# Moving output transfers, weight conversion and broadcasts between queues in an LSH-attention + MoE kernel

## The chip, the cores and the metric

The kernel runs on one core of one Trainium2 chip. The metric is device time in microseconds (us), lower is better. Before the change three timed runs gave 1048.49, 1049.14 and 1049.36 us, so a median of 1049.14 us. The five engines each execute their own instructions in order: PE (TensorE, matmuls), DVE (VectorE), ACT (ScalarE), POOL (GpSimd) and SP (SyncE, which here only issues DMA transfers).

## The reference, cut to what matters

```python
q_bits = (np.einsum('bhsd,dk->bhsk', q, proj) > 0)       # 6 hash bits per row, k likewise
mask   = q_bucket[:, :, :, None] == k_bucket[:, :, None, :]
scores = np.where(mask, scale * q @ k.T, -1e9)           # B=4, H=8, S=768, D=64
attn   = softmax(scores)
x      = (attn @ v)  -> (B*S, H*D) = (3072, 512)
h      = x @ w_in                                        # 512 -> 2048
g      = h * np.clip(h + 3.0, 0.0, 6.0) / 6.0
out    = g @ w_out                                       # 2048 -> 512
```

All inputs are 8-byte floats on the host for the two weights and float32 for q, k and v. Products are formed from a high and a low part, so most matmuls occur in twos or threes.

## The kernel before, in words

**Attention.** There are 4 x 8 = 32 heads, and 6 steps (blocks of 128 rows) to a head, so 192 steps `k`. In step `k` PE transposes the probabilities of block `k` (L347, six transposes into `pt`), multiplies an older block by the values (L384, L385), and computes the scores of block `k + 3` (`lead`, L315, L318). DVE takes the minimum of the scores (`lowest`, L325) and makes the low parts of the transposed probabilities (L371); ACT does the exponential (L337) and the high parts (L370). Where `k` is a multiple of 6, `lead` also hashes the next head: six matmuls `z` (L275 to L277) and the bits on DVE (L286).

**Preparing the next head.** Where `k % 6 == 3`, `split_qk` (L244) rounds the raw q and k on POOL (L263) into `q1`. Three DMA transfers on SP then copy halves of `q1` to `k2`, `q2` and `k1` (`kk<-qq`, `qq<-qq`, `kk<-qq`, L264 to L266), and POOL makes the two low parts (L267, L268). The hash three steps later reads all of these. `split_v` (L301, L302) comes at `k % 6 == 5`, and `scale_q` (L242), which multiplies the freshly loaded raw q for the head after, at `k % 6 == 1`. The two accumulating output transfers of each head are issued by POOL itself (`add`, L391) at `k % 6 == 4` and `1`.

**Outputs.** `output` (L394) copies an accumulated `acc` to `y` on ACT (L412), and SP writes it to the DRAM scratch `xs` (L416): 64x512 for the first four blocks of a head, 64x256 for the last two. A transfer on SP waits, in SP's order, for the copy that fills its source. The order of PE, DVE, ACT and POOL is the order of the code; the order on SP is chosen by the scheduler by its own estimate of when each source is ready, unless `tc.issue_after` names a transfer that must stand ahead.

**Weights.** The 32 pieces of the weights (`wr`, 128x512 values of 8 bytes each, handled as pairs of 32-bit words) are turned into a high and a low float part by `convert` (L159), a generator whose every `yield` ends one step: a shift on DVE (L179), a merge of two words on DVE (L181), an absolute value with scale on ACT (L186) followed by a clamp, a second merge on DVE (L194), then the high part on ACT (L199) and four low parts of 128 columns on POOL (L203). The clamp is on POOL (L189) during attention and on DVE (L192) once the feed-forward part runs. `early` (L603) has a table that says at which step `k` each of the first four pieces takes its next conversion step; the other 28 are converted in `first_ffn` (L640).

**Batch 0 is alone.** Steps 0 to 51 (48 steps of batch 0 and the first of batch 1) run without feed-forward work beside them. From step 34 on `early` also loads and normalises the finished heads for the feed-forward part: `invert`, `widen` (L572: a broadcast of 128x768 on POOL, three times), `divide` (two PE transposes `rt` and a DVE multiply, L446, L449), and transfers `load0` (`xr<-xs`, L564). `first_ffn` then runs the feed-forward part of batch 0 (48 units of 12 matmuls `h` and 6 matmuls `po`, L488 to L512). After it the remaining heads run with the feed-forward work of the batches before woven in.

## Time and profile before

| what | value |
|---|---|
| median of three timed runs | 1049.14 us |
| the profiled execution's own time | 1045.8 us |
| its span | 1043.9 us |
| mean granted PE clock | 0.996 |
| PE busy | 1009.8 us |
| DVE, ACT, POOL busy | 687.0, 584.5, 477.3 us |
| steps 12 to 47 of batch 0 | 42.73 to 144.74 us of the span |
| feed-forward of batch 0, about | 160 to 299 us |

A row of the timeline reads: start in us from the span's start, duration, engine and line, operation, output<-inputs, shape, count, and in brackets the idle time of the engine just before and what ended it. A row on windows gives for a stretch its length and then the busy time and instruction count of each engine, the granted PE clock (1.00 is full), and the share of the DMA engines. The waits view sums idle time by who waited and for whom.

### The profile page before, as it was taken

What the parts mean: (1) busy time and instruction counts of PE and PEld (TensorE: products, weight loads), DVE (VectorE), ACT (ScalarE), POOL (GpSimd) and SP (SyncE); (2) the same over time, 40 slices, a digit from 0 to 9 for tenths busy, and PEclk for the clock granted to TensorE, in tenths of its full rate; (3) what the DMA queues carried; (4) which work ended last, traced back from release to release, by engine and by line L of the source; (5) the groups of instructions that cost most, each with busy time, mean ns of one, the idle gap of its engine ahead of it and who ended that gap; (6) DMA issues with size and microseconds to landing.
All of it is one profiled execution on the core that took longest, in us unless ns stands there. A gap on an engine that the chain in (4) does not pass through costs nothing.

```text
span 1043.9 us, 18989 instructions
## 1 busy us (share of the span) xinstructions
PE 1009.8 (97%) x6846; PEld 926.0 (89%) x6846; DVE 687.0 (66%) x1441; ACT 584.5 (56%) x1308; POOL 477.3 (46%) x529
## 2 busy tenths in 40 slices
PE   8988889999999999999999999999999999999998
PEld 7977878888889998899999999999999999899996
DVE  6997888898769998766566665656665663333332
ACT  6876775556578887654554555454455462333332
POOL 5786742666537776544445444544454232200100
PEclk9999999999999999999999999999999999999999
DMA  3645559300035554322222232232232011101000
GB/s 97 150 112 130 147 150 360 142 1 1 6 110 125 115 121 134 89 62 59 60 63 63 52 95 55 43 79 64 60 93 46 15 37 28 41 1 41 1 22 20
DMA packets 47412, 80.68 MB, mean 77 GB/s; under 512 B 5924, under 2 KB 27812, under 8 KB 47320
## 3 DMA queue, kind: packets, MB, share of 16 engines
q1 hardware_dynamic: 42840, 73.98, 24.1%
q0 software_dynamic: 4480, 5.51, 4.6%
q8 instruction: 54, 0.88, 0.4%
q14 instruction: 38, 0.31, 0.1%
HBM read 41.95 MB, written 18.09 MB: 58 GB/s over the span
## 4 chain that ended last, share of the span: by engine, by line
PE 86%; DVE 6%; issue 2%; ACT 2%; DMA 2%; POOL 2%; SPq 0%; DVEq 0%; POOLq 0%; ACTq 0%
PE pt L347 11%; PE h L489 8%; PE h L488 8%; PE h L490 8%; PE po L512 7%; PE po L510 7%; PE po L511 7%; PE acc L384 6%; PE acc L385 6%; PE s L315 6%; PE s L318 6%; DVE pl L371 2%; PE z L277 1%; DVE p L325 1%; DMA qq<-qq 1%
## 5 line engine op out<-in xcount | busy, mean ns | idle before, releaser
L325 DVE TENSOR_SCALAR_CACHE_REDUCE p<-s 128x768 f32<-128x768 f32 x192 | 183.6, 956 | 102.2 <-PE pt L347 96.3
L371 DVE TENSOR_TENSOR pl<-pt,ph 128x384 fp32r<-128x384 f32 x376 | 191.9, 551 | 51.0 <-ACT ph L370 49.0
L370 ACT CAST ph<-pt 128x384 fp32r<-128x384 f32 x376 | 165.8, 481 | 64.7 <-PE pt L347 52.8
L337 ACT ACTIVATE p<-p,m 128x768 f32<-128x768 f32 x192 | 179.8, 936 | 11.1 <-DVE p L325 10.7
L497 ACT ACTIVATE g<-h,three 128x256 f32<-128x256 f32 x192 | 91.6, 477 | 153.6 <-PE h L490 131.2
L347 PE MATMUL pt<-ident,p 128*128 128x128 f32 x1152 | 162.9, 275 | 11.9 <-DVE pl L371 10.3
L503 POOL TENSOR_TENSOR gl<-g,gh 128x256 fp32r<-128x256 f32 x96 | 74.6, 777 | 203.0 <-DVE gh L502 159.4
L347 PEld LDWEIGHTS pt<-ident,p 128*128 128x128 f32 x1152 | 136.9, 141 | 31.3 <-issue 7.4
L498 DVE SCALAR_TENSOR_TENSOR g<-g,h 128x256 f32<-128x256 f32 x192 | 80.7, 420 | 114.7 <-ACT g L497 112.1
L384 PE MATMUL acc<-ph,vv 128*128 128x256 f32 x564 | 152.1, 302 | 1.0 <-DVE pl L371 1.0
L488 PE MATMUL h<-xh,w 128*128 128x256 f32 x512 | 147.7, 289 | 1.2 <-ACT y L412 1.2
L489 PE MATMUL h<-xl,w 128*128 128x256 f32 x512 | 143.3, 280 | 0.3 <-DVE xl L480 0.3
L490 PE MATMUL h<-xh,w 128*128 128x256 f32 x512 | 143.2, 280 | 0.0
L385 PE MATMUL acc<-pl,vv 128*128 128x256 f32 x564 | 140.5, 282 | 0.0
L510 PE MATMUL po<-w,gh 128*128 128x512 f32 x320 | 126.7, 396 | 0.1
L512 PE MATMUL po<-w,gl 128*128 128x512 f32 x320 | 126.5, 395 | 0.0
L511 PE MATMUL po<-w,gh 128*128 128x512 f32 x320 | 126.1, 394 | 0.0
L384 PEld LDWEIGHTS acc<-ph,vv 128*128 128x128 f32 x564 | 107.0, 190 | 2.2 <-DVE pl L371 1.9
L385 PEld LDWEIGHTS acc<-pl,vv 128*128 128x128 f32 x564 | 107.4, 190 | 0.0
L315 PE MATMUL s<-kk,qq 76*128 76x384 f32 x384 | 101.7, 346 | 2.3 <-ACT kk L291 1.5
L318 PE MATMUL s<-kk,qq 128*128 128x384 f32 x384 | 100.7, 343 | 0.0
L488 PEld LDWEIGHTS h<-xh,w 128*128 128x128 f32 x512 | 96.4, 188 | 3.8 <-ACT y L412 2.4
(137 smaller groups left out, 2025.2 us busy)
## 6 DMA issues: line engine op xcount, KB each, us to landing
raw<-in_qkT SPq DMA_DIRECT2D x32, 384.0 KB, 3.4
kk<-qq SPq DMA_DIRECT2D x62, 192.0 KB, 3.2
wr<-in_w_in SPq DMA_DIRECT2D x16, 512.0 KB, 9.6
wr<-in_w_out SPq DMA_DIRECT2D x16, 512.0 KB
vr<-in_v SPq DMA_DIRECT2D x32, 192.0 KB, 3.0
qq<-qq SPq DMA_DIRECT2D x31, 192.0 KB, 3.1
out<-ob SPq DMA_DIRECT2D x11, 512.0 KB, 3.0
xr<-xs SPq DMA_DIRECT2D x9, 512.0 KB
```

Source lines behind the costliest of these rows:

```text
L325: nc.vector.tensor_scalar(out=pr_[:], in0=s[:, :, :HW], scalar1=CAP, scalar2=None, op0=ALU.min, op1=ALU.min, accum_out=m[:],)
L337: nc.scalar.activation(pr_[:], pr_[:], AF.Exp, bias=m[:], scale=-1.0, accum_out=sms[b][:, t, h : h + 1])
L347: nc.tensor.transpose(pt[:, x], probs[g][0][:, c, x * P : (x + 1) * P], ident[:])
L371: nc.vector.tensor_sub(lo[:, :, w], pt[:], hi[:, :, w].bitcast(F32))
L384: nc.tensor.matmul(acc[:], lhsT=vv[:, kt], rhs=hi[:, x], start=(kt == 0), stop=False)
L385: nc.tensor.matmul(acc[:], lhsT=vv[:, kt], rhs=lo[:, x], start=False, stop=(kt == KT - 1))
L488: nc.tensor.matmul(hp[:], lhsT=wi[:, 0, wc], rhs=xh, start=(cc == 0), stop=False)
L489: nc.tensor.matmul(hp[:], lhsT=wi[:, 0, wc], rhs=xl, start=False, stop=False)
L490: nc.tensor.matmul(hp[:], lhsT=wi[:, 1, wc], rhs=xh, start=False, stop=(cc == NCC - 1))
L510: nc.tensor.matmul(po[u], lhsT=gh[:, us], rhs=wo[:, 0], start=(fc == 0), stop=False)
L511: nc.tensor.matmul(po[u], lhsT=gh[:, us], rhs=wo[:, 1], start=False, stop=False)
L512: nc.tensor.matmul(po[u], lhsT=gl[:, us], rhs=wo[:, 0], start=False, stop=(fc == NFC - 1))
```

## The change

Four edits go together; the numbers of matmuls and of DMA transfers stay the same.

1. Every output transfer on SP (L416) is placed behind the last of the three `q1` copies of the head split most recently (`tc.issue_after(copied.ins)`).
2. The conversion table of batch 0 has steps only at `k % 6` equal to 0, 2 and 3, two of them (0 and 2) with DVE or POOL work. Three pieces are converted whole, with seven steps, and the fourth only up to its second step; `first_ffn` starts it at its third (`stage = {WA - 1: 2}`). The high part on ACT and the four low parts on POOL become two separate steps during attention.
3. The clamp is always on DVE.
4. `widen` runs on ACT instead of POOL, at steps 36, 37 and 38 instead of 36, 38 and 42.

```diff
@@ convert
-            nc.scalar.activation(hf, hf, AF.Abs, scale=2.0 ** -112)
-        early = not ffn_on
-        if early:
-            nc.gpsimd.tensor_single_scalar(hf, hf, E_HI, op=ALU.min)
         yield
-        if not early:
-            nc.vector.tensor_single_scalar(hf, hf, E_HI, op=ALU.min)
-            yield
+        nc.vector.tensor_single_scalar(hf, hf, E_HI, op=ALU.min)
+        yield
...
         nc.scalar.copy(w[:, 0], hf)
+        if not ffn_on:
+            yield
@@ split_qk
         dma(out=k1[:D].bitcast(F32), in_=q1[D:].bitcast(F32))
+        copied = last
@@ output
-            dma(out=to, in_=outs[i][r])
+            with tc.issue_after(copied.ins):
+                dma(out=to, in_=outs[i][r])
@@ widen
-        nc.gpsimd.tensor_copy(
+        nc.scalar.copy(
             over[cc].rearrange("p (k h d) -> p k h d", k=KT, h=P // D),
@@ early
-        for n, ks in enumerate(((9, 10, 12, 13, 14), (15, 16, 18, 19, 20), (21, 22, 24, 25, 26), (27, 28, 30, 31, 32))):
+        for n, ks in enumerate(((12, 14, 15, 18, 20, 21, 24), (24, 26, 27, 30, 32, 33, 36), (36, 38, 39, 42, 44, 45, 50), (48, 50))):
...
-        put(37, div(0, 0))
-        put(38, lambda: widen(1), div(1, 0))
+        put(37, lambda: widen(1), div(0, 0))
+        put(38, lambda: widen(2), div(1, 0))
@@ first_ffn
-        stage = {}
+        stage = {WA - 1: 2}
```

**On SP, around the split at step 21.** Before, in SP's own order (`y_0` is a head's first four blocks, `y_2` its last two; `kk_975` and `qq_976` belong to the head being split):

```order
L76 DMA vr_863<-in_v 128x384
L76 DMA wr_914<-in_w_in 128x4x256
L76 DMA xs_125<-y_0_988 64x512
L76 DMA kk_975<-qq_976 64x768
L76 DMA qq_976<-qq_976 64x768
L76 DMA kk_975<-qq_976 64x768
L76 DMA raw_1051<-in_qkT 128x768
```

With the change, at the same place (the same head is `kk_959`, `qq_960`):

```order
L76 DMA xs_125<-y_2_899 64x256
L76 DMA wr_902<-in_w_in 128x4x256
L76 DMA kk_959<-qq_960 64x768
L76 DMA qq_960<-qq_960 64x768
L76 DMA kk_959<-qq_960 64x768
L76 DMA xs_125<-y_0_972 64x512
L76 DMA raw_1033<-in_qkT 128x768
```

The 64x512 output moved from ahead of the three copies to behind them; the load of the next raw head stays behind it. The same holds at the splits of steps 27 and 33. At the split of step 45 the transfer that moved behind the copies is `xr<-xs`.

**On POOL, from the split at step 21 to that at step 27.** Before:

```order
L268 TENSOR_TENSOR qq_976<-raw_827,qq_976 64x768
L391 DMA xs_125<-y_2_910 64x256
L301 CAST vv_1048<-vr_863 128x6x64
L302 TENSOR_TENSOR vv_1048<-vr_863,vv_1048 128x6x64
L189 TENSOR_SCALAR wr_914<-wr_914 128x512
L391 DMA xs_125<-y_0_988 64x512
L242 TENSOR_SCALAR raw_1051<-raw_1051 64x768
L203 TENSOR_TENSOR w_990<-wr_914,w_990 128x128 x4
L263 CAST qq_1200<-raw_1051 128x768
```

With the change (line numbers are shifted by up to 6: L272 is L268 of before, L395 is L391, L305 and L306 are L301 and L302, L266 is L263):

```order
L272 TENSOR_TENSOR qq_960<-raw_817,qq_960 64x768
L395 DMA xs_125<-y_2_899 64x256
L305 CAST vv_1030<-vr_853 128x6x64
L306 TENSOR_TENSOR vv_1030<-vr_853,vv_1030 128x6x64
L203 TENSOR_TENSOR w_652<-wr_471,w_652 128x128 x4
L395 DMA xs_125<-y_0_972 64x512
L242 TENSOR_SCALAR raw_1033<-raw_1033 64x768
L266 CAST qq_1181<-raw_1033 128x768
```

The clamp is gone, and the four low parts of a piece no longer stand right ahead of the split; they stand behind `split_v`, and in every second head only.

**On DVE, from the bits at step 12 on.** Before (L194 is the second merge of the first piece, L179 the shift of the second):

```order
L286 TENSOR_SCALAR qq_528<-z_641,thr,val 44x768
L325 TENSOR_SCALAR p_667,m_666<-s_648 128x768
L371 TENSOR_TENSOR pl_0_632<-pt_0_657,ph_0_631 128x3x128
L371 TENSOR_TENSOR pl_1_636<-pt_1_661,ph_1_635 128x3x128
L194 SCALAR_TENSOR_TENSOR wr_471<-wr_471 128x512
L325 TENSOR_SCALAR p_702,m_701<-s_680 128x768
L371 TENSOR_TENSOR pl_0_712<-pt_0_692,ph_0_711 128x3x128
L371 TENSOR_TENSOR pl_1_716<-pt_1_696,ph_1_715 128x3x128
L325 TENSOR_SCALAR p_739,m_738<-s_719 128x768
L371 TENSOR_TENSOR pl_0_712<-pt_0_729,ph_0_711 128x3x128
L371 TENSOR_TENSOR pl_1_716<-pt_1_733,ph_1_715 128x3x128
L179 TENSOR_SCALAR wr_690<-wr_690 128x512
```

With the change (L290 is the bits, L329 is L325, L375 is L371, L181 is the shift and L183 the first merge of the first piece):

```order
L290 TENSOR_SCALAR qq_528<-z_638,thr,val 44x768
L181 TENSOR_SCALAR wr_471<-wr_471 128x512
L329 TENSOR_SCALAR p_664,m_663<-s_645 128x768
L375 TENSOR_TENSOR pl_0_629<-pt_0_654,ph_0_628 128x3x128
L375 TENSOR_TENSOR pl_1_633<-pt_1_658,ph_1_632 128x3x128
L329 TENSOR_SCALAR p_698,m_697<-s_677 128x768
L375 TENSOR_TENSOR pl_0_708<-pt_0_688,ph_0_707 128x3x128
L375 TENSOR_TENSOR pl_1_712<-pt_1_692,ph_1_711 128x3x128
L183 SCALAR_TENSOR_TENSOR wr_471<-wr_471 128x512
```

The shift moved from the step in which POOL splits (step 15) to behind the bits (step 12), and merges stand at step `k % 6 == 2` alone.

## The prediction

> **What bounds the kernel now.** I read the page first (PE busy 97% of the span), so only PE's idle time and time at a lower clock can be won. Then the windows, one per head of batch 0, cut at the first transposes of a head. The columns are the stretch, its length, busy time of PE, weight loads, DVE, ACT, POOL, the PE clock, DMA share.

> ```profile
> core 0 of [0], span 1043.9 us
> core 0: us, PE busy (x) PEld busy (x) DVE busy (x) ACT busy (x) POOL busy (x), PEclk, DMA share, GB/s
> 28.84:42.73 13.89, 13.79 (x104) 13.28 (x102) 13.22 (x28) 11.81 (x27) 9.49 (x9) 1.00 0.62 152
> 42.73:58.57 15.84, 13.97 (x104) 13.29 (x102) 15.38 (x31) 13.04 (x29) 13.20 (x14) 1.00 0.55 135
> 58.57:74.41 15.84, 13.96 (x104) 13.30 (x102) 15.28 (x30) 13.17 (x29) 13.16 (x14) 1.00 0.43 99
> 74.41:92.79 18.38, 14.44 (x104) 13.28 (x102) 15.37 (x31) 13.02 (x29) 13.14 (x14) 1.00 0.57 146
> 92.79:111.50 18.71, 15.83 (x103) 14.74 (x102) 13.26 (x29) 13.16 (x30) 11.59 (x12) 0.91 0.45 115
> 111.50:129.42 17.92, 15.40 (x111) 14.03 (x110) 14.05 (x32) 12.46 (x28) 13.55 (x14) 1.00 0.67 171
> 129.42:144.74 15.32, 14.44 (x109) 13.63 (x107) 14.57 (x31) 13.17 (x31) 12.10 (x12) 1.00 0.54 138
> 318.69:332.35 13.66, 13.66 (x104) 13.29 (x102) 12.58 (x26) 11.88 (x28) 9.84 (x9) 1.00 0.51 120
> ```

> The same work takes 13.66 us in an undisturbed head of batch 1 (last row) and 13.89 in the second head of batch 0, but 15.3 to 18.7 in the six heads in which weights are converted and batch 0 is normalised. These six heads last 102.01 us together; six of 13.66 would be 81.96. What PE waited for from 42.73 to 160 us, by the waits view:

> ```profile
> PE pt L347 <- DVE pl L371: 8.2, 10, 1.6
> PE z L276 <- DMA kk<-qq: 6.1, 4, 2.0
> PE z L277 <- DMA qq<-qq: 1.8, 3, 0.7
> ```

> So there are two causes of like size: DVE is late with the low parts, and the hash waits for the copies of `q1`. The second has its explanation on POOL and SP (step 27; POOL, then SP, then PE):

> ```profile
> 84.79 1.75 POOL L203 TENSOR_TENSOR w<-wr,w 128x128 fp32r<-128x128 f32 x4 [1.97 <-PE pt L347]
> 86.50 0.82 POOL L263 CAST qq<-raw 128x768 fp32r<-128x768 f32 x1
> 92.67 0.47 SPq L76 DMA_DIRECT2D xs<-y  x1
> 93.24 0.54 SPq L76 DMA_DIRECT2D kk<-qq  x1
> 96.56 0.39 PE L276 MATMUL z<-kk,pjh 128*108 128x384 f32 x1 [2.02 <-DMA kk<-qq]
> ```

> The copy's source was ready at 87.32, yet SP issued it at 93.24, right behind an output that had to wait for its `y`. On top of that L263 started 1.75 us late, behind the low parts of a weight piece. DVE's own lateness shows here:

> ```profile
> 47.90 2.14 POOL L242 TENSOR_SCALAR raw<-raw 64x768 f32<-64x768 f32 x1
> 48.70 0.68 DVE L194 SCALAR_TENSOR_TENSOR wr<-wr 128x512 uint32<-128x512 uint32 x1
> 50.87 0.41 PE L347 MATMUL pt<-ident,p 128*128 128x128 f32 x2 [0.32 <-DVE pl L371]
> 53.17 1.84 POOL L267 TENSOR_TENSOR kk<-raw,qq 64x768 fp32r<-64x768 f32 x1
> 53.25 2.04 DVE L179 TENSOR_SCALAR wr<-wr 128x512 uint32<-128x512 uint32 x1
> 165.35 0.42 DVE L179 TENSOR_SCALAR wr<-wr 128x512 uint32<-128x512 uint32 x1
> 169.97 0.42 DVE L192 TENSOR_SCALAR wr<-wr 128x512 f32<-128x512 f32 x1
> ```

> The shift L179 takes 2.04 us when it starts beside POOL's L267, and 0.42 us at 165.35, where POOL has nothing. The clamp on DVE (L192) also takes 0.42 us alone. A single merge of 0.68 us costs PE 0.32 us two steps on.

> **Heads of steps 12 to 35.** They took 15.84 + 15.84 + 18.38 + 18.71 = 68.77 us. Of that go:
> - the waits for copies at steps 24 and 30 (parts of the 6.1 and 1.8 above): the copies are issued when L263 ends, some 6 us before the hash, and L263 no longer stands behind L203. At steps 12 and 18, where the copies were ahead already, no wait for them is in the view, so nothing is next there at once;
> - the long shifts: they move to where POOL has no split, so 0.42 instead of 2.04 us;
> - a third of the DVE steps: two a head (0.42 and 0.68, together 1.10 us) instead of three (2.04, 0.68 and 0.68, together 3.40).

> The nearest head is that of 28.84 (13.89 us), which holds one shift and one merge and no late copy. If every merge costs PE its 0.32 us and the short step is hidden, a head takes 13.98; if the short step costs as much again, 14.3; if both lie in DVE's slack, 13.66. I take 14.0, near the measured head: 56.0 us, so **-12.8** (bounds -11.6 and -14.1).

> In this sum the clock counts too:

> ```profile
> 97.10:100.50 3.40, 3.00 (x11) 2.88 (x12) 1.09 (x1) 0.00 (x0) 2.10 (x2) 0.57 0.63 144
> ```

> Granted clock 0.57 for 3.40 us, right after the 2.02 us wait of 96.56, costs some 1.5 us. I let it go with the wait. [...] The row has the drop right behind the longest gaps and nowhere else in these heads, so I follow the row.

> Merges at `k % 6 == 2` may meet POOL's L242. The row of 48.70 lies wholly inside L242's (47.90 to 50.04) and took 0.68 us, as does a merge alone; I count nothing. [...]

> **Head of steps 36 to 41** (17.92 us). The copies' wait goes here as well. Added: three `widen` on ACT at the ends of steps 36 to 38, and the first merge and an absolute value. The nearest rows for their cost:

> ```profile
> L189 POOL TENSOR_SCALAR wr<-wr 128x512 f32<-128x512 f32 x4 | 6.3, 1566 | 7.0 <-ACT wr L186 7.0
> L575 POOL COPY lent<-rc 128x768 f32<-128x768 f32 x3 | 2.5, 818 | 0.0
> L337 ACT ACTIVATE p<-p,m 128x768 f32<-128x768 f32 x38 | 35.7, 938 | 6.1 <-DVE p L325 5.9
> L186 ACT ACTIVATE wr<-wr 128x512 f32<-128x512 f32 x4 | 2.7, 674 | 0.0
> L446 PE MATMUL rt<-ident,lent 128*128 128x128 f32 x12 | 2.3, 271 | 0.0
> ```

> An ACT pass over 768 columns is 0.94 us, so 2.8 us go to ACT within three steps; POOL had 0.82 each in its idle time, where they cost nothing. PE's own need is 13.66 plus four divides of two transposes (2.3 us / 6 = 0.38 each), 15.2 us. ACT was busy 12.46 us in this head, and 12.46 + 2.8 + 0.7 (L186) = 16.0. ACT so becomes the later one; with its burst at the head's start I take 16.8 (bounds 15.2 and 17.9), so **-1.1** (-2.7 to 0).

> **Head of steps 42 to 47** (15.32 us). DVE is busy 14.57 us and gets a clamp and a merge, 1.1 us; some hides. PE's floor is 13.66 + 2 x 0.38 = 14.4. I take 15.9, **+0.6** (-0.9 to +1.1).

> **Steps 48 to 51.** The hash of 48 waits for copies that stand behind a transfer waiting on DVE; later PE waits for DVE:

> ```profile
> 142.85 0.38 SPq L76 DMA_DIRECT2D xr<-xs  x1
> 143.32 0.48 SPq L76 DMA_DIRECT2D kk<-qq  x1
> 147.68 0.39 PE L276 MATMUL z<-kk,pjh 128*108 128x384 f32 x1 [0.49 <-DMA kk<-qq]
> 153.31 0.52 PE L347 MATMUL pt<-ident,p 128*128 128x128 f32 x3 [1.42 <-DVE pl L371]
> ```

> The copies now go ahead of `xr`; the waits of 0.49 and at most 0.7 (longest of its kind) go. The fourth piece's shift and merge, 0.42 + 0.68, fall on DVE just where PE waits for it. **-0.1** (-1.2 to +1.1).

> **Start of the feed-forward part.** The fourth piece brings one pass on DVE of 0.42 and one of 0.68, two on ACT and L203 on POOL (1.75) into its first four units. At 165.97 PE already runs without a margin:

> ```profile
> 165.97 0.50 PE L510 MATMUL pos<-w,gh 128*128 128x512 f32 x1
> ```

> It followed the high part of `g` by less than one pass. I take **+0.75** (0 to +1.8), between nothing and the two DVE passes plus one of ACT. Steps 9 to 11 lose their conversion steps, **-0.2** (0 to -0.2). From there on the order on every queue is that of before.

> **The sum.** -12.8 - 1.1 + 0.6 - 0.1 + 0.75 - 0.2 = -12.85 us. The profiled execution took 1045.8 us (span 1043.9), so 1032.95; the median shown stands 3.34 us above that execution, and I carry this along: 1049.14 - 12.85 = 1036.3 us. All lower bounds together give -19.1 (1030.0), all upper ones -7.6 (1041.5), and with a clock drop that stays -6.1 (1043.0).

> **Rivals.**
> - *All cover holds.* Every short step lies in slack and each head takes PE's floor. For it: DVE is busy only 12.58 of 13.66 us in the undisturbed head. Against: 0.32 us behind one merge. 1030 to 1031.5. Chance 0.15.
> - *POOL and DVE still meet.* The shifts and clamps at `k % 6 == 0` fall beside `split_v`, or beside L203, now put there at steps 24 and 36, and take 2.04 us again: 1.6 us in six heads, 9.7 us. [...] Either way 1045 to 1047.5. Against: POOL sat idle 7.0 us in four waits right ahead of L189 (row above), 1.75 each, at the place of the shifts; L203 is four pieces of 0.44, so a meeting there costs a piece; and the row of 48.70. [...] Chance 0.08.
> - *Slower: a loop through SP and POOL.*

> ```profile
> raw<-in_qkT SPq DMA_DIRECT2D x32, 384.0 KB, 3.4
> ```

>   The raw load of the next head stands behind the output, the output behind the copies, the copies behind L263, and the next L263 behind L242 of that raw load. If this loop is longer than a head, every head takes the loop's time. From rows of step 27: 0.82 for L263, 5.35 from its end (87.32) to the output (92.67), 0.5 for the output's issue, 3.4 until raw has landed, 2.14 for L242: 12.2 of 13.66 us. It decides above that. To end slower it must first eat 13 us in six heads, 2.2 us a head, so be 16 us long; at 16.3 the time is near 1052. Against: the raw load stood behind the same output before. Chance 0.04.
> - *ACT becomes the bound beyond step 41.* The three passes push the exponentials and the delay isn't caught up until the hash of 48: 2 to 3 us more, 1038.5 to 1039.5. Chance 0.13.
> - [...] Chance 0.08.

> My forecast keeps 0.52 and covers 1032 to 1040. The range that leaves out no more than two in ten is **1031 to 1042.5**: it loses the second and third rival and part of the first. About 0.2% (2.1 us) is what a measurement of this kernel can tell from no change. Faster by more than that: 0.52 + 0.15 + 0.13 + 0.08 and half of the second rival, 0.92; within it the other half, 0.04; slower 0.04.

> **What would show it.** Right: no idle time of `z` for DMA from 42 to 150 us; SP's `kk<-qq` within 1 us of L263's end at steps 21, 27, 33, 45; L179 and the clamp at 0.4 to 0.7 us; heads 12 to 35 at 13.7 to 14.3 us, the head of 36 at 16 to 17.5; clock 1.00 throughout. Wrong: a wait for copies that is still there, L242 waiting for its raw load until past the third step, shifts of 2 us, or an ACT with no idle time from 36 to 47 and PE waiting for `p`.

## The result, and the profile after

| | before | after |
|---|---|---|
| median of the timed runs | 1048.82 us (4 runs, 1044.79 to 1049.36) | 1032.83 us (4 runs, 1031.71 to 1035.13) |
| ratio, 95% interval | | 0.9859 (0.9828 to 0.989) |
| the profiled execution | 1045.8 us | 1033.77 us |
| its span | 1043.9 us | 1031.6 us |
| its mean granted PE clock | 0.996 | 0.995 |

The change took 16.0 us off the median, and 12.3 us off the span of the profiled executions. Measured once more (e11 below), the two medians lay 13.7 us apart. Two disturbed runs (5612.97 us of the first experiment, 1409.6 us of before) are left out of all that follows.

The windows of after, cut at the first transposes of a head as those of before were: steps 6, 12, 18, 24, 30, 36, 42, and in the last row step 48 up to the feed-forward part.

```profile
28.13:41.78 13.65, 13.65 (x103) 13.29 (x102) 12.55 (x26) 11.86 (x28) 9.38 (x8) 1.00 0.58 153
41.78:55.98 14.20, 13.95 (x104) 13.30 (x103) 13.68 (x28) 12.48 (x29) 10.40 (x9) 1.00 0.63 151
55.98:70.18 14.20, 13.96 (x103) 13.36 (x102) 13.68 (x28) 12.44 (x29) 10.16 (x8) 1.00 0.64 152
70.18:84.94 14.76, 14.04 (x103) 13.35 (x102) 14.23 (x28) 12.45 (x29) 11.77 (x12) 1.00 0.72 182
84.94:99.15 14.21, 13.97 (x104) 13.35 (x102) 13.70 (x28) 12.46 (x29) 10.15 (x9) 1.00 0.61 152
99.15:115.59 16.44, 15.56 (x111) 13.98 (x110) 15.93 (x34) 14.82 (x32) 12.79 (x13) 1.00 0.62 150
115.59:132.28 16.69, 14.63 (x109) 13.68 (x107) 16.31 (x33) 13.74 (x32) 11.68 (x11) 1.00 0.65 164
132.28:147.00 14.72, 12.35 (x81) 11.00 (x82) 11.87 (x27) 8.12 (x20) 3.31 (x8) 0.88 0.53 155
```

Heads 12 to 35 went from 68.77 to 57.37 us (-11.40), the head of step 36 from 17.92 to 16.44 (-1.48), that of step 42 from 15.32 to 16.69 (+1.37). Steps 48 to 51 with the feed-forward part came out even (154.68 to 154.70), all behind them too (744.51 to 744.62), and the start with steps 0 to 11 came out 0.95 us shorter. Of that, 0.24 us lie in the head of step 6 (13.89 to 13.65); the rest is the first six steps, whose end lies anywhere from 27.37 us (e1) to 29.20 us (e2) in the profiled executions here, so that part is chance. DVE's busy time tells where the price lies: 16.31 of 16.69 us in the head of step 42.

The waits of PE from 41.78 to 160 us in after:

```profile
PE pt L351 <- DVE pl L375: 3.5, 3, 1.8
PE acc L388 <- DVE pl L375: 2.1, 6, 0.6
PE acc L388 <- DVE late L455: 0.5, 1, 0.5
PE pt L351 <- DVE lent L375: 0.4, 1, 0.4
PE pos L516 <- ACT gh L508: 0.2, 1, 0.2
```

No `z` is among them: the 7.9 us in which the hash waited for copies are gone, and what is left is nearly all DVE. The cause shows at the split of step 27, on POOL and SP:

```profile
78.49 0.82 POOL L266 CAST qq<-raw 128x768 fp32r<-128x768 f32 x1 [2.38 <-PE s L322]
79.34 0.49 SPq L76 DMA_DIRECT2D kk<-qq  x1
```

The cast ends at 79.31 and the first copy is issued at 79.34. Before, 5.92 us lay between the two.

### The profile page after: what moved, and what is told of

Its sections match the earlier page's. It is cut to its first block, busy times and chain, and to the rows that moved or that the text cites. A ratio compares the mean times of both kernels' runs of the same rounds, so it can differ in the third digit from the quotient of the medians.

```text
span 1031.6 us, 19001 instructions
## 1 busy us (share of the span) xinstructions
PE 1007.9 (98%) x6846; PEld 925.8 (90%) x6846; DVE 688.2 (67%) x1445; ACT 585.2 (57%) x1311; POOL 470.4 (46%) x522
## 4 chain that ended last, share of the span: by engine, by line
PE 80%; DVE 12%; ACT 3%; issue 3%; DMA 1%; POOL 0%; DVEq 0%; POOLq 0%; ACTq 0%
PE pt L351 10%; PE h L495 7%; PE h L494 7%; PE h L496 7%; PE po L516 7%; PE po L518 7%; PE po L517 7%; PE acc L388 6%; PE acc L389 6%; PE s L319 5%; PE s L322 5%; DVE pl L375 2%; DVE p L329 2%; DVE qq L290 1%; PE z L281 1%
## 5 line engine op out<-in xcount | busy, mean ns | idle before, releaser
L329 DVE TENSOR_SCALAR_CACHE_REDUCE p<-s 128x768 f32<-128x768 f32 x192 | 183.5, 955 | 99.8 <-PE pt L351 95.4
L375 DVE TENSOR_TENSOR pl<-pt,ph 128x384 fp32r<-128x384 f32 x376 | 191.7, 550 | 50.7 <-ACT ph L374 48.9
## 6 DMA issues: line engine op xcount, KB each, us to landing
raw<-in_qkT SPq DMA_DIRECT2D x32, 384.0 KB, 3.5
```

The costliest lines, as they stand in the source:

```text
L329: nc.vector.tensor_scalar(out=pr_[:], in0=s[:, :, :HW], scalar1=CAP, scalar2=None, op0=ALU.min, op1=ALU.min, accum_out=m[:],)
L375: nc.vector.tensor_sub(lo[:, :, w], pt[:], hi[:, :, w].bitcast(F32))
```

## What the conversion steps cost now

DVE's steps of a piece (L181 the shift, L183 and L192 the merges, L190 the clamp) and the POOL instructions that stand beside them, in after:

```profile
45.69 0.43 DVE L181 TENSOR_SCALAR wr<-wr 128x512 uint32<-128x512 uint32 x1
45.73 2.37 POOL L242 TENSOR_SCALAR raw<-raw 64x768 f32<-64x768 f32 x1 [0.49 <-DMA raw<-in_qkT]
63.72 0.82 POOL L266 CAST qq<-raw 128x768 fp32r<-128x768 f32 x1 [0.30 <-PE s L322]
63.96 1.12 DVE L192 SCALAR_TENSOR_TENSOR wr<-wr 128x512 uint32<-128x512 uint32 x1
73.98 2.14 POOL L242 TENSOR_SCALAR raw<-raw 64x768 f32<-64x768 f32 x1 [0.33 <-DMA raw<-in_qkT]
74.09 0.99 DVE L181 TENSOR_SCALAR wr<-wr 128x512 uint32<-128x512 uint32 x1
119.46 2.18 POOL L242 TENSOR_SCALAR raw<-raw 64x768 f32<-64x768 f32 x1
119.50 1.11 DVE L190 TENSOR_SCALAR wr<-wr 128x512 f32<-128x512 f32 x1
```

The merges at step `k % 6 == 2` did not take 0.68 us: in heads 12 to 35 the four took 1.11 to 1.13. They now start 0.24 to 0.25 us behind the start of POOL's cast L266, which moved forward when L203 left its place. The shift or clamp takes 0.43 us where it starts ahead of L242, and about 1 us where it starts just behind it. In both late rows it ends 1.10 to 1.15 us after L242's start, while L242's record runs for 2.14 us. So a shift or clamp just behind L242's start was held up for some 0.7 us (1.10 less its own 0.43), not for the 2.14. Sixteen shifts and clamps in the traces of after and its variants (e2 to e6, e10, e11) start 0.01 to 0.48 us into an L242 of 2.14 us, and every one ends 1.10 or 1.11 us after L242's start.

Such a meeting cost the head about what it cost the shift. The head of step 24 took 14.76 us where its neighbours took 14.20, and its shift 0.99 where their shift or clamp took 0.43: 0.56 us both times. In e10, which has the same instructions there, the shift was over before L242 started, took 0.43 us, and this head 14.19. In e11, the same kernel as after, two heads had such a meeting (shifts of 1.09 and 0.87 us) and took 14.85 and 14.64. Whether the raw load that L242 waits for lands before or after the shift differs from one execution to the next.

That is why the row of 48.70 in the prediction misled: that merge started 0.80 us into L242, behind the 0.7 us that hurt. The trace of before holds a second meeting of the same two instructions, which the prediction passed over. There the merge started 0.45 us into L242 and took 0.93 us:

```profile
64.09 2.14 POOL L242 TENSOR_SCALAR raw<-raw 64x768 f32<-64x768 f32 x1 [0.44 <-DMA raw<-in_qkT]
64.54 0.93 DVE L194 SCALAR_TENSOR_TENSOR wr<-wr 128x512 uint32<-128x512 uint32 x1
```

The merges beside the cast took 0.44 us longer where the cast still had 0.58 us to go (63.96 to 64.54). It went the other way round too: the subtraction L271 takes 2.15 us where it starts while such a merge still runs (50.43, merge until 50.88), and 1.83 or 1.84 us in e4 and e7, where none does. The shifts beside L242 were over while L242's record ran on for another 1.0 us; whether L242 let go of DVE that early or its record on POOL runs on past its work, the trace can't say.

## The experiments

Each was timed against before in runs on the same chip. Lengths are those of the profiled executions, by head as above.

**e1, the first edit alone**, to see how the gain divides between the copies' order and DVE's steps.

```diff
 (before)
+        copied = last            # in split_qk, behind the third copy
...
-            dma(out=to, in_=outs[i][r])
+            with tc.issue_after(copied.ins):
+                dma(out=to, in_=outs[i][r])
```

> The kernel before with the first edit alone: output transfers stand behind the copies of the split on SP, nothing else. Theory (two causes of like size, which partly hide each other): the waits of the hash for copies at steps 24, 30, 36 and 48 go (8.4 us in the profile of before, and the half clock after them), but DVE, which caught up in those waits, now shows its own lateness: heads of steps 12 to 35 at 61 to 65 us instead of 68.8, whole kernel 5 to 9 us faster than before. Rival A (DVE alone is the bound, copies were hidden behind it): 0 to 3 us faster. Rival B (copies alone; the table of steps adds nothing): 11 us faster or more, as fast as the whole change.

Measured: 1034.36 us (three runs, 1034.11 to 1035.68), ratio 0.9869 (0.9845 to 0.9894). Windows of steps 12 to 47:

```profile
41.24:57.06 15.82, 13.95 (x104) 13.28 (x102) 15.39 (x31) 13.04 (x29) 13.19 (x14) 1.00 0.55 135
57.06:72.90 15.84, 13.97 (x104) 13.31 (x102) 15.13 (x30) 13.02 (x29) 13.14 (x14) 1.00 0.56 136
72.90:88.66 15.76, 13.92 (x104) 13.27 (x102) 15.34 (x29) 13.14 (x29) 13.11 (x14) 1.00 0.63 171
88.66:102.81 14.15, 13.84 (x103) 13.31 (x102) 13.26 (x29) 13.10 (x30) 11.64 (x12) 1.00 0.60 151
102.81:117.82 15.01, 15.01 (x111) 14.06 (x110) 14.03 (x32) 12.43 (x28) 13.49 (x14) 1.00 0.65 165
117.82:133.17 15.35, 14.47 (x108) 13.65 (x107) 14.57 (x31) 13.16 (x31) 12.19 (x12) 1.00 0.56 139
```

The first edit alone brings 11.7 of the 12.3 us of the span. Counted from step 6 on, without the start that differs by chance, it is 10.2 of 11.6, of which 10.1 lie in the heads of steps 24, 30 and 36 (55.01 to 44.92 us). The heads of steps 12, 18 and 24 stay at 15.8, with shifts of 2.05, 1.71 and 1.67 us beside the subtraction. PE's wait for DVE is what it was before (8.2 us):

```profile
PE pt L351 <- DVE pl L375: 8.1, 10, 1.6
```

Heads 12 to 35 took 61.57 us, inside the 61 to 65 of my expectation, but the kernel gained 13.6 us on before where it said 5 to 9: it was missed, and the rival that gives the copies' order the whole is nearer. The other edits win 1.6, 1.6 and 1.0 us in the heads of steps 12, 18 and 24, and pay 1.43 and 1.34 us back in those of steps 36 and 42, where before had no conversion left.

**e2, the change without its first edit** (the table, the clamp and `widen` as in after):

```diff
 (after)
-            with tc.issue_after(copied.ins):
-                dma(out=to, in_=outs[i][r])
+            dma(out=to, in_=outs[i][r])
```

> The changed kernel without its first edit: the table, the clamp and the broadcasts are as changed, and the order of the output transfers on SP is left to the scheduler again. On SP the outputs stand behind the copies even so; only the transfer xr<-xs stands ahead of the copies at the split of step 45. Theory (edits 2 to 4 make the scheduler choose nearly the order that edit 1 forces): the heads of steps 12 to 35 as with the change, 57.4 us together, and the hash of step 48 waits 0.9 to 1.9 us for copies again; kernel 0.5 to 2 us slower than the changed one, so 11 to 13 us faster than before. Rival (edit 1 carries the gain in this kernel too): the waits at steps 24, 30 and 36 are back, heads of steps 12 to 41 longer by 6 to 8 us.

Measured: 1033.86 us, ratio 0.9865 (0.9842 to 0.9889), the heads within 0.2 us of those of after but for the first, and no wait for copies. At the split of step 21 SP has the first copy ahead of the output by itself:

```profile
65.61 0.47 SPq L76 DMA_DIRECT2D kk<-qq  x1
71.09 0.46 SPq L76 DMA_DIRECT2D xs<-y  x1
```

At the split of step 45 `xr` stood behind the copies too, so the wait that I expected at step 48 did not come. The scheduler, with the other three edits in the code, chooses this order itself (presumably because the cast, no longer behind L203, is ready earlier by its estimate; which of the three does it wasn't tried). So the order of SP is a result of those edits as much as of the first: either alone does it.

**e3, `widen` back on POOL**, to see whether ACT's three passes make the head of step 36 long:

```diff
 (after)
-        nc.scalar.copy(
+        nc.gpsimd.tensor_copy(
...
-        put(37, lambda: widen(1), div(0, 0))
-        put(38, lambda: widen(2), div(1, 0))
+        put(37, div(0, 0))
+        put(38, lambda: widen(1), div(1, 0))
... (the third at 42)
```

> The changed kernel with the three broadcasts back on POOL at steps 36, 38 and 42. Theory (in the head of steps 36 to 41 DVE is the late engine, not ACT): that head stays within 0.4 us of 16.44 and the whole kernel within 1 us. Rival (the burst of three ACT passes is what makes this head longer than its floor of 15.2 us, as the prediction had it): the head falls to 15.2 to 15.8 us, the kernel is 0.7 to 1.3 us faster.

Measured: 1035.11 us, ratio 0.9873 (0.9851 to 0.9894). ACT's busy time in the head of step 36 fell from 14.82 to 13.20 us, but the head did not get shorter. Its window, and a wait of PE in it:

```profile
101.40:118.10 16.70, 15.32 (x112) 14.06 (x111) 16.12 (x33) 13.20 (x30) 12.79 (x12) 1.00 0.58 151
```

```profile
105.51 0.52 PE L351 MATMUL pt<-ident,p 128*128 128x128 f32 x3 [1.08 <-DVE pl L375]
```

DVE is busy 16.12 of 16.70 us. The head is DVE's; the prediction's ACT theory fell. In e1, where `widen` is on POOL too and no conversion step is left in this head, it takes 15.01 us. The kernel did not stay within 1 us of after's 1032.83: in this build SP has `xr` ahead of the copies of step 45 again, and step 48 takes 5.76 us instead of 3.87.

**e4, the merges one step earlier** (`k % 6 == 1`, away from the cast):

```diff
 (after)
-((12, 14, 15, 18, 20, 21, 24), (24, 26, 27, 30, 32, 33, 36), (36, 38, 39, 42, 44, 45, 50), (48, 50))
+((12, 13, 15, 18, 19, 21, 24), (24, 25, 27, 30, 31, 33, 36), (36, 37, 39, 42, 43, 45, 50), (48, 49))
```

> The changed kernel with the two merges of each piece (and the fourth piece's one) one step earlier, at k % 6 equal to 1 instead of 2, so that on DVE they come beside the later part of POOL's scale_q and no longer beside the rounding of the split. [...] Rival (scale_q blocks DVE for its whole 2.14 us): merges of 1.3 to 2.2 us, heads longer than 58 us, kernel 1 to 5 us slower than the changed one.

Measured: 1034.24 us, ratio 0.9864 (0.9838 to 0.989). The four merges of heads 12 to 35 did shrink, and the heads did not (two of the four):

```profile
48.41 0.68 DVE L183 SCALAR_TENSOR_TENSOR wr<-wr 128x512 uint32<-128x512 uint32 x1
62.80 0.68 DVE L192 SCALAR_TENSOR_TENSOR wr<-wr 128x512 uint32<-128x512 uint32 x1
```

Heads 12 to 35 took 58.67 us (14.39, 14.41, 14.81, 15.06) against 57.37 in after and the 55.5 to 56.6 that I expected. Part of the difference is that two heads here have a shift or a clamp right behind L242's start (0.84 and 1.08 us; heads of 14.81 and 15.06), and after has one. But the two heads without such a meeting are 0.2 us longer than after's as well. My theory, that a head pays the 0.44 us by which a merge is longer, fell. That DVE has less slack right behind the shift and the bits than a step later is the reading that is left; it wasn't tried by itself.

**e5, the clamp on POOL during attention, and e6, the same with `xr` behind the copies.**

```diff
 (after; e5)
-        nc.vector.tensor_single_scalar(hf, hf, E_HI, op=ALU.min)
+        (nc.vector if ffn_on else nc.gpsimd).tensor_single_scalar(hf, hf, E_HI, op=ALU.min)
 (e6 as well, in load0)
+        with tc.issue_after(copied.ins) if t == 2 else ExitStack():
             dma(out=xr0[t]..., in_=xs[0]...)
```

> The changed kernel with the clamp of the attention part back on POOL, at the same steps 18, 30 and 42. Theory (POOL rests there and DVE is the late engine in these heads): the heads of 18 and 30 shorter by 0 to 0.3 us each, that of 42 by 0.5 to 1.1 us, kernel 0.5 to 1.5 us faster than the changed one. Rival (the clamp of 1.6 us on POOL pushes scale_q and with it the next split): the heads after steps 18, 30 and 42 longer, kernel 0.5 to 2 us slower.

> The changed kernel with the clamp back on POOL, and the last xr<-xs transfer held behind the copies of the split of step 45, which the run with the clamp alone had lost. Theory: as with the clamp alone, heads of 18 and 30 at 14.0 us and that of 42 at 15.9, and step 48 at 3.9 us instead of 6.1: 1 to 1.5 us faster than the changed kernel. Rival (the wait at 48 only hid DVE's lateness in steps 49 to 51): steps 48 to 51 no shorter than with the clamp alone, kernel as fast as the changed one or slower.

Measured: e5 1034.48 us, 0.9863 (0.9841 to 0.9884); e6 1032.14 us, 0.9847 (0.9819 to 0.9876). The heads with a clamp got shorter in both: in e5 14.04 (step 18), 14.03 (30) and 15.87 (42) against 14.21, 14.21 and 16.69. But in e5 the scheduler put `xr` in front of the copies at step 45, which the first edit does not forbid (it names the outputs alone); the hash of step 48 waited again, and the kernel gained nothing. SP and PE of e5:

```profile
129.29 0.38 SPq L76 DMA_DIRECT2D xr<-xs  x1
129.76 0.48 SPq L76 DMA_DIRECT2D kk<-qq  x1
134.54 0.39 PE L280 MATMUL z<-kk,pjh 128*108 128x384 f32 x1 [0.92 <-DMA kk<-qq]
135.87 0.40 PE L281 MATMUL z<-qq,pjh 128*108 128x384 f32 x1 [0.93 <-DMA qq<-qq]
```

In e6 the copies go first, over 4 us earlier:

```profile
125.18 0.48 SPq L76 DMA_DIRECT2D kk<-qq  x1
129.57 0.39 SPq L76 DMA_DIRECT2D xr<-xs  x1
```

Both waits are gone, step 48 is back from 6.14 to 3.87 us, and the heads keep their gain. By the medians e6 is 0.7 us faster than after and not the 1 to 1.5 expected; their ranges overlap, so that lead isn't shown. The pair shows the same wait that the change removed come and go by one transfer's place on SP.

**e7, e8, e9: other ways to keep conversion off the subtractions, on top of e1.** All three start from e1 (two merges and a shift a head, four pieces done by step 32, nothing in heads 36 and 42). e7 moves only the shift to `k % 6 == 0`, with the pieces loaded a head earlier. e8 adds e6's edit of `xr`. e9 moves the first merge from `k % 6 == 4` to 2 as well.

```diff
 (e1, the table)
-((9, 10, 12, 13, 14), (15, 16, 18, 19, 20), (21, 22, 24, 25, 26), (27, 28, 30, 31, 32))
+((6, 10, 12, 13, 14), (12, 16, 18, 19, 20), (18, 22, 24, 25, 26), (24, 28, 30, 31, 32))   # e7, e8
+((6, 8, 12, 13, 14), (12, 14, 18, 19, 20), (18, 20, 24, 25, 26), (24, 26, 30, 31, 32))    # e9
```

> The kernel before with the first edit and one thing more: the shift of each piece (DVE) stands at k % 6 equal to 0 (steps 6, 12, 18, 24) instead of 3, apart from POOL's split; the pieces are loaded one head earlier for it. All else, one piece a head, clamp and broadcasts on POOL, is as before. Theory (what is left in the heads of 12 to 29 after the first edit, 15.8 us each, is the shift of 2.05 us; the number of DVE steps costs little): these heads at 14.2 to 14.7 us, the heads of 36 and 42 as with the first edit alone (15.0 and 15.35), kernel 3 to 5 us faster than the first edit alone and 2 to 4 faster than the whole change. Rival (the number of conversion steps in a head costs, wherever they stand): these heads at 15.2 to 15.8 us, kernel 0 to 2 us faster than the first edit alone.

> As the run with the shift apart, with the last xr<-xs transfer held behind the copies of the split of step 45. Theory: the hash of step 48 waits no more (0.96 us with the first edit alone), so 0.5 to 1 us faster than without; a version that beats both kernels, near 1028 to 1031 us. Rival (steps 48 to 51 are DVE's): no faster than without.

> As the run with the shift apart and xr behind the copies, with the first merge of each piece also moved, from k % 6 equal to 4 (where it took 2.01 us beside POOL's second subtraction of the split) to 2. Theory (not the number of DVE steps costs, but what of them stands beside the two subtractions of the split): merges of at most 1.15 us, the heads of 12, 18 and 24 at 14.5 to 15.0 us instead of 15.8 to 15.9, kernel 2 to 3.5 us faster than that run, near 1031 to 1033 us; it beats the changed kernel by 0.5 to 2 us. Rival (the number of steps): these heads at 15.4 to 15.9 us, kernel less than 1 us faster.

Measured: e7 1036.14 us, 0.989 (0.9865 to 0.9914); e8 1035.0, 0.9875 (0.9853 to 0.9896); e9 1031.34, 0.9854 (0.9833 to 0.9875). e7 was 1.8 us slower than e1 where 3 to 5 us faster was expected, and e8 missed the 1028 to 1031 us of its expectation by 4 us, though step 48 fell from 6.07 (e7) to 3.88 us. In e7 the shifts fell to 0.60 us and the heads of steps 18 and 24 stayed at 15.86, which looked like the rival's case, three DVE steps a head being too many. The trace of e7 has another reason:

```profile
55.50 1.83 POOL L272 TENSOR_TENSOR qq<-raw,qq 64x768 fp32r<-64x768 f32 x1
55.88 2.01 DVE L181 SCALAR_TENSOR_TENSOR wr<-wr 128x512 uint32<-128x512 uint32 x1
```

The merge now ran into the second subtraction and took 2.01 us in the shift's stead (a merge alone: 0.68). e9 takes it away from there:

```profile
50.29 2.19 POOL L203 TENSOR_TENSOR w<-wr,w 128x128 fp32r<-128x128 f32 x4 [0.81 <-DMA xs<-y]
50.95 0.79 DVE L181 SCALAR_TENSOR_TENSOR wr<-wr 128x512 uint32<-128x512 uint32 x1
```

With the same three steps a head, heads 12 to 35 took 14.59, 14.88, 14.84 and 14.27 us, 58.58 together; in e8 they were 14.59, 15.88, 15.88 and 15.50, 61.85. What counted here is which POOL instruction stands beside a step, and the rival fell. The third step still seems to cost something: 14.9 us with three against 14.2 with two, though part of this is the shift, which takes 0.82 to 0.83 us beside POOL's clamp in the two heads of 14.9. Heads 36 and 42 are free of conversion, 15.01 and 15.76, but the head of step 6, into which it moved, takes 14.79 us where e1 has 13.87 and after 13.65.

**e10, PE made to idle.** The cheap way to settle the clock: after, with DVE's minimum repeated at three blocks of the middle, where there are no other gaps. The result of a repetition is the same.

```diff
 (after, lowest)
+        for _ in range({80: 4, 110: 5, 140: 6}.get(g, 0) + 1):
             nc.vector.tensor_scalar(...)
```

> The changed kernel with the minimum of the scores done 5, 6 and 7 times over (4, 5 and 6 repeats, same result) at the blocks 80, 110 and 140, in the quiet part of the trace, so that PE idles there for some us. [...] Rival (the half clock comes by chance or by load): no half clock there, or half clock elsewhere.

Measured in one execution: 1051.65 us, span 1049.6. Windows that hold the three gaps (3.40, 3.32 and 4.50 us), each with what follows it; the granted clock is the number behind POOL's count:

```profile
348.27:351.68 3.41, 0.41 (x3) 0.07 (x1) 3.31 (x7) 0.00 (x0) 2.21 (x2) 1.00 0.71 185
351.68:358.51 6.83, 6.43 (x27) 6.27 (x27) 4.26 (x9) 3.58 (x8) 0.76 (x1) 0.50 0.07 15
437.02:440.43 3.41, 0.25 (x3) 0.04 (x1) 3.31 (x9) 0.49 (x2) 0.00 (x0) 1.00 0.28 77
440.43:443.84 3.41, 3.25 (x9) 2.89 (x10) 1.57 (x6) 1.03 (x2) 1.66 (x3) 0.50 0.00 0
597.44:600.86 3.42, 0.15 (x2) 0.00 (x0) 3.31 (x7) 0.47 (x1) 0.47 (x1) 1.00 0.29 77
600.86:607.68 6.82, 5.59 (x18) 4.93 (x19) 2.70 (x9) 1.38 (x3) 3.72 (x3) 0.50 0.11 12
```

Each window in which PE was busy for 0.15 to 0.41 us is followed by half clock, for one or two windows, and from 144 to 1048 us the clock drops nowhere else. The gaps make 11.2 us and the half of 17.1 us at half clock 8.5, so 19.7 together; the span is 18.0 us longer than that of after. So idle time of PE cost twice here: the 11.2 us themselves, and by this count up to 8.5 us in the one or two windows behind each gap.

**e11 and e12, after and the kernel of e9 once more, side by side.**

> The changed kernel once more, unaltered, so that the next kernel can be set beside it in runs of one chip. Theory (step 48 to 51 of the changed kernel still loses about 1.3 us to a half clock, and heads 36 and 42 pay 1.4 and 1.3 us for conversion beside the divides): 1032 to 1034.5 us. Rival (its first four timed runs were low by chance): 1035 to 1036.

> The kernel of e9 once more, with five rounds, beside the changed kernel. Theory (all four pieces done by step 32, no two-input subtraction beside VectorE's conversion): 1.5 to 2.5 us below the changed kernel, as the spans of the profiles say (1029.3 against 1031.6). Rival (the lead in the profile is the spread of single runs, 1 us in the start alone): within 0.7 us of it.

Measured: after 1033.07 us (1032.71 to 1033.29), ratio 0.9864 (0.9839 to 0.9888); the kernel of e9 1031.79 us (1030.92 to 1032.22), 0.9851 (0.983 to 0.9872). All four runs of the one lie below all four of the other, by 1.28 us in the median: a lead, less than the theory's 1.5 and more than the rival's 0.7. The spans are 1031.4 and 1029.7. So the kernel with the first edit, `xr` behind the copies and a table that starts no DVE step inside the two subtractions beats after by about a thousandth. (e6 has the lowest ratio to before, 0.9847, and was not set beside it.) In this pair the heads 12 to 35 of e9's kernel are 0.8 us longer than those of after, and its head of step 6 is 1.1 us longer; it gains 1.4 us each in heads 36 and 42, and 1.5 us from step 48 to the end of the feed-forward part, where no half clock falls.

## Why the prediction was right, and where not

The forecast was 1036.3 us with a range of 1031 to 1042.5; 1032.83 was measured, and 1033.07 in the repetition. Its mechanism, waits for copies removed and shifts moved out of the subtractions, is what the runs show; that the number came so near is in part luck, as terms missed in both directions. Of its signs, the wait of `z` is gone, and the first copy is issued 0.02 to 0.03 us after the cast's end at all four splits it named. Three of the six shifts and clamps in heads 12 to 47 lie above the 0.4 to 0.7 us it gave, one head above 14.3, and the clock did not stay at 1.00. Its steps by themselves:

- **Heads 12 to 35, forecast -12.8, measured -11.40.** The heads came out at 14.20, 14.20, 14.76 and 14.21 where 14.0 was taken. Of the missing 1.4 us, 0.56 are the shift's meeting with L242 in the head of step 24. The sum has no term for it: it took every shift at 0.42 us. The other 0.2 a head fit the "short step" that 14.0 leaves nearly hidden: where it is gone from DVE (e5, heads of 18 and 30), 14.04 and 14.03 are left. "I count nothing" for a merge beside POOL was wrong as a length, 1.12 us and not 0.68: it rested on the row of 48.70 and passed over that of 64.54, and the meeting that came was with the cast of the split. But those two heads of e5 have merges of 1.08 and 1.06 us, and e4 shows that a shorter merge does not make the head shorter by itself. So most of the 1.4 us is not the merges' doing; how much of it is stays open.
- **How the gain divides.** The prediction had "two causes of like size". e1 has nearly all of the gain in the copies' order alone, with DVE's waits as they were. The rest of the change is worth its 4.3 us in heads 12 to 29 less the 2.8 us of heads 36 and 42, little more than the spread of the runs.
- **Head of step 36, forecast -1.1, measured -1.48.** The size was right and its reason wrong. "ACT so becomes the later one" failed: without ACT's passes the head is 16.70 us (e3). DVE, which the sum for this head leaves out, is the later one, with a shift of 0.75 and a merge of 1.25 us beside the divides.
- **Head of step 42, forecast +0.6, bound +1.1, measured +1.37.** Mis-sized: the clamp took 1.11 us beside L242 and the merge 0.98, 2.1 us where 1.1 was counted. e5 takes the clamp off DVE and the head falls by 0.82 us, to 15.87.
- **Steps 48 to 51 and the feed-forward start, forecast +0.65 together, measured +0.02.** Three things offset each other. Step 48 went from 5.52 to 3.87 us, more than the 1.2 of the copies' waits; why more was not traced. Step 50 got 0.34 us longer, with the fourth piece's shift on DVE. The start of the feed-forward part lost 1.34 us, but not for the reason given. In e4, where no half clock falls there, the same stretch takes 144.64 us against 144.58 before, so the fourth piece's passes cost next to nothing where +0.75 was taken. The 1.34 are the clock.
- **Steps 9 to 11, forecast -0.2, measured -0.24** in the head of step 6.
- **The clock.** "I let it go with the wait" was half right: the half clock at 97.6 us went, and another came at 140.96. The two windows of each kernel, after first, then before:

```profile
137.55:140.96 3.41, 1.66 (x14) 1.28 (x11) 3.08 (x9) 1.48 (x4) 2.78 (x7) 1.00 0.31 90
140.96:144.37 3.41, 3.37 (x16) 2.88 (x15) 2.55 (x6) 1.51 (x4) 0.00 (x0) 0.50 0.87 267
```

```profile
94.19:97.61 3.42, 0.85 (x5) 0.39 (x4) 1.35 (x4) 2.05 (x5) 2.18 (x2) 1.00 0.97 247
97.61:101.02 3.41, 3.41 (x13) 3.26 (x14) 1.09 (x1) 0.07 (x1) 2.11 (x2) 0.50 0.50 98
```

  In after PE waits 1.75 us for DVE at 139.53, in a window in which it is idle for 51% (1.66 of 3.41 us busy). In e10 the starts of half clock, 351.68, 440.43 and 600.86 us, lie 26 and 47 times 3.413 us apart, and half clock lasted one or two such stretches. The stretch ahead of it was not always idle throughout: PE was busy for 4 to 12% of it in e10, for 25% in before and for 49% in after. What decides near one half stays open, since in e4 the stretch from 137.91 to 141.32 us (counted back by 3.413 us from its half clock at 1032.20) has the same 1.66 of 3.41 us busy and no half clock behind it.
- **The carry to the median.** The 3.5 us by which the time came out lower lie in none of these terms, whose sum was -12.85 against -12.33 in the profile. They lie in "the median shown stands 3.34 us above that execution, and I carry this along". That excess is not fixed. After's median lies 0.94 us below its own profiled execution. Over the 29 runs of before that stood beside the experiments, time and granted clock go together (correlation -0.87), at 0.69 us for each 0.001 of clock:

```
run of before, us   1044.61  1045.81  1047.72  1049.54  1051.02
granted clock        0.998    0.996    0.994    0.991    0.991
```

  The profiled execution had 0.996, the median run of these 0.994 (1047.40 us; 12.85 less would be 1034.55); eight timed runs of after had 0.995 to 0.999. A run of before that loses more windows at its waits loses them no more when the waits are gone. That these runs' half clocks lie at those waits is argued from e10 and the profiled one; only one execution of before was traced.

Of the rivals, none is the case. *POOL and DVE still meet* happened in kind but at 0.3 to 0.7 us a meeting, not 1.6. The *loop through SP and POOL* did not close, but came near: L242 waits for its raw load 0.3 to 1.8 us in heads 12 to 35. It ends 0.30 us ahead of the cast in the head of step 18 (63.42, cast at 63.72), where that wait is longest, and 1.4 to 2.4 us ahead in the others, and the cast itself waits for PE. *ACT as the bound* fell with e3. No run shows a clock drop that stays, the 1.5 us in the bound of 1043.0: the half clock at 97.6 us went, and one of 1.34 us came at another place, in the stretch behind PE's wait of 1.75 us for DVE.

## What to carry to other kernels

Look first at what stands ahead of a late transfer in its queue; one constraint on the order brought here nearly what the whole change did (e1), the reshuffle brought the same order without it (e2), and a scheduler may put another transfer ahead as soon as the code around it changes (e3, e5). In these runs a shift that takes 0.42 us alone took up to 2.05 us (e1) and a merge of 0.68 us up to 2.03 us (e7), by the POOL instruction beside it; so price a step on VectorE by the GpSimd instruction that will stand beside it at its new place, not by its own length or by one lucky row. Spreading work into a stretch that had none must be charged at that stretch's slack: the change won 4.3 us and paid 2.8 for it, while e9 won 3.0 us over e1 in heads 12 to 35 and paid 0.9 in the head of step 6 and 0.4 in that of step 42 (nothing there in e12).
